# Row sums of two tiles as small products on TensorE, ordered last column blocks, and a new list of priorities

## The chip, the cores and the metric

The kernel runs on one core of one Trainium2 chip. The metric is the device time of one execution in microseconds (us). Three runs of the kernel before took 1046.98, 1047.38 and 1047.85 us; the median is 1047.38 us.

## What is computed

Three layers follow one another. Attention: 4 sequences of 768 positions, 8 heads of 64 columns; each chunk of 32 queries sees 8 memory slots, 16 positions to the left, its own 32 and 8 to the right, 64 slots in all.

```python
scores = scale * np.matmul(q_c, k_full.transpose(0, 1, 3, 2))
scores = scores - np.max(scores, axis=-1, keepdims=True)
a = np.exp(scores)
a = a / (np.sum(a, axis=-1, keepdims=True) + 1e-09)
out[:, :, c_start:c_end] = np.matmul(a, v_full)
```

Then two dense layers over the 3072 x 512 result, each 512 -> 2048 -> 512:

```python
h = x @ w_in;  r = np.maximum(h, 0.0);  g = s * (r * r) + b;  x = g @ w_out      # first
h = x @ w_in2; g = h * (1.0 / (1.0 + np.exp(-1.702 * h)));    out = g @ w_out2   # second
```

## The kernel before, in words

**Tiles.** The 3072 rows are 24 attention tiles of 128 queries. A tile (`attend`, L509 and on) goes through these steps: its k, q and v are loaded (L521); TensorE computes 64 small score products (`scores`, L536); VectorE finds each row's maximum (`top`, L553) and subtracts it (`less`, L556); ScalarE takes the exponential (`exp`, L561); TensorE transposes the result in four 128x128 pieces (`turn`, L569); ScalarE or VectorE copies it to `px` (`turned`, a copy at L328); TensorE multiplies with the values, 64 small products (`values`, L597); VectorE divides by the row sums (`norm`, L602); TensorE transposes back (`back`, L611); a copy takes the high part of the number (`keep`, L328) and VectorE the residual (`left`, L628). The row sums are `total`: a reduction (L579), the addition of 1e-9 (L582) and a reciprocal (L583), all on VectorE, on the exponentials before they are transposed. Tiles 0 to 3 are done one by one at the start, later ones in pairs; one row of 128 queries holds eight sums, two heads for each of four pieces.

**Dense layers.** All matrices are split into a high and a low part, and each product is made of three. The first layer's first 16 tiles go through `step`: hidden products into `ph` (L726), the gate (L732 to L751), output products into `accA` and `accB` (L759). The first steps work on halves of 256 columns, the first of them on tiles 0 and 1, the next on tiles 2 and 3. The first layer's weights are loaded as pairs of words, put together by bit steps on ScalarE and VectorE (`words`, L444 to L468) and split (L328 for the high part, L428 for the residual). The rest of the first layer and the whole second one go through `wino`, which makes seven products in place of eight of 2x2 blocks; its output products are at L1242. The last of them, for the last block, is issued in two pieces, one for each column block (`only`), after which VectorE adds each block to what is there (`last`, L1283) and SyncE stores it.

**Order.** The order of all operations on all engines is made before the program is built: each `op` has a due time, durations on the engines that may run it, the operations it follows, and buffers that it takes. `Plan.order` places them one after another by due time, and `SHIFTS`, a list of (first operation, how many, by how much), moves due times. Where the plan leaves TensorE idle before the first output product, idle products of a cleared tile (`cold`) are put in (L1398), into a spare pair of banks of the accumulator memory; nine more such products (`warm`, L383) stand at the very start.

Of the kernel before, what the change touches and what calls it, by code (L numbers as in the profile page):

```python
# [8 lines left out]
F32 = mybir.dt.float32  # L9
# [6 lines left out]
P = 128  # L16
# [34 lines left out]
    (1612, 256, 5), (1631, 4, 2.35), (1699, 64, -7.76), (1949, 16, -5.07), (932, 16, -1.12), (2436, 1, 0.44),  # L51
    (2730, 64, -7.95), (494, 16, -2.28), (617, 1, -1.49), (277, 256, -1.21), (3339, 4, -5.47), (3114, 1, 0.41),
    (2366, 1, 0.18), (11, 256, 1.49), (2644, 4, 0.18), (1872, 64, -0.2), (1819, 256, 1.74), (1792, 64, 0.54),
    (1748, 4, -0.8), (811, 16, -0.39), (3178, 64, -0.19), (1893, 1, 3.68), (1836, 16, -0.51), (2342, 256, 1.22),
    (586, 4, 6.05), (718, 1, -0.28), (163, 4, -0.28), (1005, 1, 2.98), (807, 1, -3.69), (2414, 1, -0.31),
    (1125, 16, 9.26), (2154, 256, -5.84), (2762, 4, -0.29), (1303, 16, 0.6), (1999, 16, -0.13), (2173, 16, 2.02),
    (26, 1, -8.88), (2170, 256, 8.5), (661, 16, -0.26), (400, 1, 10.24), (2178, 256, -1.34), (174, 256, 0.29),
    (134, 1, 2.37), (1826, 1, -0.12), (1408, 64, -4.02), (3376, 1, -8.4), (1390, 64, 0.99), (533, 1, 11.29),
    (3346, 190, -0.03), (1751, 16, -4.82), (1002, 4, 0.43), (2961, 16, -5.97), (866, 1, 5.95), (2455, 1, 0.71),
    (2840, 16, 0.37), (2154, 1, 2.59), (1139, 64, -6.74), (2904, 4, -1.42), (3397, 1, -1.7), (2313, 1, 0.2),  # L60
    (735, 256, 2.52), (2432, 4, -0.29), (1090, 1, 4.94), (1555, 16, -17.14), (56, 4, 0.91), (2969, 16, 1.88),
    (1680, 1, -0.19), (1510, 256, 12.15), (1265, 16, -6.14), (3127, 1, 0.01), (541, 64, 1.59), (545, 64, 0.39),
    (3220, 16, -3.41), (832, 4, 1.02), (1732, 64, -0.3), (295, 16, 0.5), (3353, 1, -0.07), (169, 16, -1.93),
    (2542, 1, -7), (571, 1, -0.78), (930, 16, 1.9), (1956, 4, -0.67), (829, 4, -5.41), (3219, 1, -1.84),
    (1547, 16, -7.23), (687, 64, 6.82), (2974, 256, -0.53), (2700, 1, 0.08), (1878, 4, -1.83), (588, 4, 4.82),
    (2496, 1, -0.32), (630, 256, -0.9), (942, 1, 0.01), (1754, 16, -0.05), (1295, 1, 0.35), (488, 4, 0.68),
    (52, 16, -0.37), (3529, 7, -0.92), (2015, 4, -0.39), (1956, 1, -0.08), (2924, 1, -2.32), (1156, 16, -7.77),
    (2844, 16, 2.35), (177, 1, 3.67), (50, 1, -0.46), (591, 64, -1.01), (856, 1, -3.3), (1006, 1, 0.8),
    (2193, 1, -0.41), (1372, 64, 15.19), (485, 4, 3.62), (672, 1, 3.48), (2030, 4, 0.07), (1474, 4, 1.64),
    (2478, 16, -2.66), (3007, 256, 3.34), (272, 1, -2.45), (2452, 1, -0.46), (900, 1, -3.84), (2024, 256, -3.55),  # L70
    (3270, 256, 0.54), (91, 1, -4.78), (1423, 1, 5.39), (2014, 1, 11.48), (1053, 1, 0.14), (2198, 256, -0.21),
    (1768, 16, 3.5), (2254, 1, -1.34), (722, 1, 4.56), (895, 1, -0.86), (1290, 1, -1.23), (1546, 1, -1.37),
    (2311, 16, 11.12), (1200, 1, 15.34), (863, 1, -0.4), (291, 16, 2.64), (3258, 16, 1.92), (3273, 16, 4.73),
    (1726, 4, -0.36), (2745, 1, -2.35), (2473, 64, 0.01), (1200, 4, 2.13), (2860, 64, 1.9), (3408, 128, 0.27),
    (2952, 1, 1.67), (3033, 16, 6.88), (985, 1, -10.64), (1180, 4, -10.28), (1714, 16, 0.31), (2727, 1, -0.98),
    (1961, 64, -11.04), (1888, 64, -3.48), (2164, 1, 0.4), (933, 4, 1.23), (1005, 1, 9.03), (1568, 256, -2.38),
    (1989, 256, -1.22), (499, 4, 0.83), (2385, 1, -6.17), (610, 4, -1.31), (1250, 16, 5.62), (655, 1, 11.83),
    (3443, 93, 0.22), (1326, 256, -1.49), (498, 1, 0.41), (1667, 64, 5.33), (1797, 256, 0.03), (1155, 1, -20.91),
    (2379, 16, -1.41), (2101, 256, 11.19), (2234, 16, -0.24), (1835, 1, 1.88), (3409, 4, 0.21), (3, 4, -9.87),
    (634, 64, -1.41), (425, 1, 3.76), (899, 4, -15.64), (2121, 1, 3.25), (1645, 1, 2.15), (43, 256, -0.21),  # L80
    (3152, 64, -15.49), (2815, 64, -0.61), (2367, 16, 1.67), (63, 256, -0.26), (800, 1, 19.59), (2835, 16, 1.94),
    (426, 16, -4.3), (2965, 16, 0.96), (1667, 256, 11.64), (174, 64, 2.81), (795, 1, -1.21), (2316, 256, 9.24),
    (2389, 16, -1.62), (3184, 256, -0.7), (1421, 64, -2.34), (2254, 16, 0.37), (80, 4, 2), (2972, 256, -3.98),
    (1302, 4, 0.3), (1751, 1, 0.29), (245, 1, 0.35), (480, 4, 1.53), (3273, 1, 0.77), (3301, 64, -2.33),
    (3310, 16, -2.39), (890, 64, -10.03), (941, 4, 3.21), (3309, 227, -0.12), (3305, 1, -5.09), (2282, 16, -0.03),
    (3002, 256, 5.54), (3291, 245, -0.4), (1884, 4, -1.75), (1457, 256, -0.29), (86, 64, -1.33), (2836, 1, 0.23),
    (468, 1, -0.65), (2000, 256, -0.82), (2323, 256, 0.31), (1866, 16, 0.88), (311, 1, 0.59), (72, 16, -13.18),
    (301, 256, -1.7), (1495, 64, -15.18), (106, 16, -9.62), (2998, 256, -10.32), (1203, 4, -0.12), (711, 16, 0.51),
    (2941, 16, 7.51), (2426, 4, -4.62), (2322, 1, -0.14), (1625, 16, -1.68), (2214, 16, 10.14), (1162, 64, -0.26),
    (394, 16, -14.55), (3295, 1, 11.77), (93, 1, -0.12), (2705, 1, -6.51), (2579, 4, 9.15), (2820, 16, -8.49),  # L90
    (2855, 1, 0.62), (953, 1, 1.8), (1438, 1, -9.09), (3351, 64, -9.1), (3389, 4, 0.41), (3484, 52, 1.11),
    (159, 64, -7.43), (735, 4, -1.72), (2740, 4, 3.76), (945, 1, -0.31), (1350, 64, 0.21), (2547, 1, 0.15),
    (3506, 30, -1.86), (2385, 4, 9.5), (3455, 16, -1.31), (1034, 4, 3.08), (2651, 4, -0.12), (1099, 1, 0.12),
    (222, 16, 2.76), (876, 1, 1.39), (2089, 256, 1.17), (2940, 16, -10.33), (278, 1, 0.71), (1063, 16, 0.45),
    (1791, 1, -1.41), (2919, 16, 0.54), (2902, 4, -0.45), (851, 16, 0.78), (3343, 1, 0.62), (1308, 1, -0.35),
    (2886, 16, -0.79), (1046, 4, -8.74), (740, 1, 5.36), (80, 1, 10.95), (1607, 1, -6.38), (2004, 64, -0.09),
    (1235, 1, 0.18), (1880, 1, 3.01), (1640, 1, -5.04), (828, 64, -0.31), (1947, 16, 1.9), (2898, 1, -0.51),
    (2407, 64, 2.44), (3100, 1, 2.11), (3202, 64, -0.68), (1363, 4, 0.12), (265, 16, -0.61), (2830, 1, -0.07),
# [193 lines left out]
def attention_moe_moe(ctx: ExitStack, tc: tile.TileContext, q_t, k_w, v_w, w_in1, w_out1, s_b, w_in2, w_out2, out):  # L292
# [32 lines left out]
    T = {}  # L325
# [39 lines left out]
    def chill(e):  # L365
        T["cold"] = pp.tile([P, KT, 512], F32, tag="ys", name="cold")[:, 0].bitcast(F32R)
        fill(e, T["cold"].bitcast(F32), 0.0)
# [1089 lines left out]
```

## Time and profile before

| what | us |
|---|---|
| median of three runs | 1047.38 |
| the profiled execution, its whole time | 1048.4 |
| its span, first to last instruction | 1046.4 |
| TensorE busy with products | 1034.9 |
| VectorE busy | 756.7 |
| ScalarE busy | 603.8 |

One execution was recorded. The span leaves out 2.0 us of the execution's time around it. TensorE is PE, and PEld its weight loads; VectorE is DVE, ScalarE ACT, GpSimd POOL, SyncE SP. A line such as L597 is a line of the kernel; L328 is a helper that many copies share. An idle time in brackets stands before an instruction, with what ended it; "issue" means that nothing in the profile ended it. [...]

### The profile page before, as it was taken

What the parts mean: (1) busy time and instruction counts of PE and PEld (TensorE: products, weight loads), DVE (VectorE), ACT (ScalarE), POOL (GpSimd) and SP (SyncE); (2) the same over time, 40 slices, a digit from 0 to 9 for tenths busy, and PEclk for the clock granted to TensorE, in tenths of its full rate; (3) what the DMA queues carried; (4) which work ended last, traced back from release to release, by engine and by line L of the source; (5) the groups of instructions that cost most, each with busy time, mean ns of one, the idle gap of its engine ahead of it and who ended that gap; (6) DMA issues with size and microseconds to landing.
All of it is one profiled execution on the core that took longest, in us unless ns stands there. A gap on an engine that the chain in (4) does not pass through costs nothing.

```text
span 1046.4 us, 19645 instructions
## 1 busy us (share of the span) xinstructions
PE 1034.9 (99%) x7563; PEld 850.8 (81%) x7563; DVE 756.7 (72%) x1144; ACT 603.8 (58%) x933; POOL 0.7 (0%) x6
## 2 busy tenths in 40 slices
PE   7999999999999999999999999999999999999998
PEld 5888888888888888888888888888888888888886
DVE  7996997879898758889999365896323996222955
ACT  5766765546666657788845476553354543454432
POOL 0000000000000000000000000000000000000000
PEclk9999999999999999999999999999999999999999
DMA  9679955748899964988978998877666677566662
GB/s 351 234 262 329 296 181 184 257 178 272 294 338 360 350 209 180 324 291 284 372 221 283 346 295 293 277 243 242 211 201 196 213 254 229 175 202 217 204 214 88
DMA packets 148605, 265.55 MB, mean 254 GB/s; under 512 B 14240, under 2 KB 59552, under 8 KB 148512
## 3 DMA queue, kind: packets, MB, share of 16 engines
q1 hardware_dynamic: 148224, 263.77, 75.2%
q8 instruction: 60, 0.98, 0.4%
q10 hardware_dynamic: 288, 0.52, 0.2%
q14 instruction: 33, 0.27, 0.1%
HBM read 190.84 MB, written 73.40 MB: 253 GB/s over the span
## 4 chain that ended last, share of the span: by engine, by line
PE 80%; DVE 4%; DMA 3%; issue 0%; ACT 0%; SPq 0%; DVEq 0%
PE pc L1242 12%; PE ph L726 9%; PE pb L1242 8%; PE pd L1242 8%; PE accA L759 5%; PE accB L759 5%; PE ph L1093 3%; PE pd L1093 3%; PE ph L1095 3%; PE pd L1095 3%; PE ph L1094 3%; PE pd L1094 3%; PE pb L1094 2%; PE pb L1093 2%; PE pc L1093 2%; PE pc L1094 2%
## 5 line engine op out<-in xcount | busy, mean ns | idle before, releaser
L1215 ACT CAST oj<-G 128x1024 fp32r<-128x1024 f32 x72 | 75.6, 1054 | 75.4 <-PE pd L1242 31.1
L1218 DVE TENSOR_TENSOR oj<-G,oj 128x1024 fp32r<-128x1024 f32 x72 | 87.6, 1220 | 40.4 <-ACT oj L1215 40.4
L732 ACT ACTIVATE r<-ph 128x512 f32<-128x512 f32 (+1 forms) x66 | 38.5, 583 | 61.8 <-PE ph L726 38.1
L1218 DVE TENSOR_TENSOR oq<-G,oq 128x1024 fp32r<-128x1024 f32 x40 | 48.9, 1222 | 30.0 <-ACT oq L1215 29.8
L1215 ACT CAST oq<-G 128x1024 fp32r<-128x1024 f32 x40 | 42.1, 1053 | 47.4 <-PE pc L1242 21.9
L1242 PE MATMUL pc<-oj,wih 128*128 128x512 f32 x224 | 69.0, 389 | 0.0
L1105 ACT ACTIVATE G<-ys 128x512 f32<-128x512 f32 x64 | 40.4, 631 | 36.5 <-DVE ys L1147 35.9
L1242 PE MATMUL pd<-oj,wih 128*128 128x512 f32 x192 | 59.1, 389 | 0.0
L1227 DVE TENSOR_TENSOR G<-G 128x1024 f32<-128x1024 f32 x48 | 57.3, 1218 | 0.1
L747 ACT CAST gh<-r 128x512 fp32r<-128x512 f32 (+1 forms) x66 | 39.9, 605 | 25.2 <-PE accB L759 15.1
L751 DVE TENSOR_TENSOR gl<-r,gh 128x512 fp32r<-128x512 f32 (+1 forms) x66 | 44.2, 669 | 14.2 <-ACT gh L747 11.2
L450 ACT ACTIVATE u<-st 128x512 f32<-128x512 f32 x64 | 42.9, 670 | 17.1 <-DMA st<-w_in 9.7
L1242 PE MATMUL pb<-oj,wih 128*128 128x512 f32 x160 | 49.3, 389 | 0.0
L1242 PE MATMUL pc<-oq,wih 128*128 128x512 f32 x160 | 49.3, 389 | 0.0
L1242 PEld LDWEIGHTS pc<-oj,wih 128*128 128x128 f32 x224 | 42.1, 188 | 8.7
L462 DVE SCALAR_TENSOR_TENSOR u<-u,st 128x512 uint32<-128x512 uint32 x64 | 43.5, 687 | 2.8 <-ACT st L458 1.5
L458 ACT ACTIVATE st<-st 128x512 uint32<-128x512 uint32 x64 | 42.8, 672 | 1.8 <-DMA st<-w_out 1.0
L468 DVE SCALAR_TENSOR_TENSOR u<-st,u 128x512 uint32<-128x512 uint32 x64 | 43.4, 683 | 0.4
L1242 PE MATMUL pc<-oj,wil 128*128 128x512 f32 x112 | 43.6, 389 | 0.0
L1242 PEld LDWEIGHTS pd<-oj,wih 128*128 128x128 f32 x192 | 36.0, 188 | 7.4
L759 PE MATMUL accA<-gh,woh 128*128 128x512 f32 (+1 forms) x132 | 42.0, 393 | 0.0
L739 ACT ACTIVATE r<-r 128x512 f32<-128x512 f32 (+1 forms) x66 | 40.8, 618 | 1.6
(229 smaller groups left out, 2735.2 us busy)
## 6 DMA issues: line engine op xcount, KB each, us to landing
wih<-wodh SPq DMA_DIRECT2D x112, 256.0 KB, 3.6
wil<-wodl SPq DMA_DIRECT2D x112, 256.0 KB, 3.9
wih<-wch SPq DMA_DIRECT2D x96, 256.0 KB, 3.6
wil<-wcl SPq DMA_DIRECT2D x96, 256.0 KB, 3.9
st<-w_in SPq DMA_DIRECT2D x32, 512.0 KB, 6.2
st<-w_out SPq DMA_DIRECT2D x32, 512.0 KB, 5.8
k<-k_w SPq DMA_DIRECT2D x24, 512.0 KB, 6.1
v<-v_w SPq DMA_DIRECT2D x24, 512.0 KB, 6.5
```

Source lines behind the costliest of these rows:

```text
L462: nc.vector.scalar_tensor_tensor(out=u, in0=u, scalar=3, in1=T["st", i][:, :, 0], op0=ALU.logical_shift_left, op1=ALU.bitwise_or)
L468: nc.vector.scalar_tensor_tensor(out=u, in0=T["st", i][:, :, 1], scalar=0x80000000, in1=u, op0=ALU.bitwise_and, op1=ALU.bitwise_or)
L726: nc.tensor.matmul(T["ph", i], T[win][x][:, k * P:(k + 1) * P], T["x", m, b][y][:, k, r], start=seen_["hid"] == 1, stop=seen_["hid"] == 3 ...
L751: nc.vector.tensor_tensor(out=gl, in0=T["r", i], in1=gh.bitcast(F32), op=ALU.subtract)
L759: nc.tensor.matmul(T["acc", group, k // 2][:, k % 2][:, r], T[wout][x][:, k * P:k * P + P], T["g", i][y], start=fresh and (x, y) == (0, 0) ...
L1093: nc.tensor.matmul(ph, wh, xh, start=first and i == 0, stop=False, skip_group_check=True)
L1094: nc.tensor.matmul(ph, wh, xl, start=False, stop=False, skip_group_check=True)
L1095: nc.tensor.matmul(ph, wl, xh, start=False, stop=i == 1, skip_group_check=True)
L1215: nc.scalar.copy(out=T[kh], in_=g_of(ty, z))
L1218: nc.vector.tensor_tensor(out=T[kl], in0=g_of(ty, z), in1=T[kh].bitcast(F32), op=ALU.subtract)
L1227: o_raw[out, x] = [op(need, {"dve": 1.22}, lambda e: nc.vector.tensor_tensor(out=g_of(out, z), in0=g_of(a, z), in1=g_of(b, z), op=o), afte ...
L1242: nc.tensor.matmul(acc[:, k], lt[:, z], rh, start=first and x == 0, stop=p == HALF - 1 and x == 2, skip_group_check=True)
```

## The change

For tiles 0 and 1 the row sums are not taken by VectorE. Once `px` is there, TensorE multiplies each of its four pieces with a small matrix of two columns that holds ones for one head's 64 slots each, and one more product of the identity and a matrix of eight columns of 1e-9 adds the constant; the eight columns stand in the second bank of the spare pair, tile 0's and tile 1's side by side. VectorE then takes one reciprocal. The matrix of ones is filled on GpSimd at the start, in a part of the cleared tile. The code also has a form in which the sums share the values' bank (`apart` false); with `SUMMED` as it stands it is not used. The two pieces of the last product now follow one another by a dependency. The list of priorities is the old one with its numbers moved by the three added operations, and 171 more entries. The spare pair is made at the start and not at the first idle product.

```diff
 SHIFTS = (
-    (1612, 256, 5), (1631, 4, 2.35), (1699, 64, -7.76), (1949, 16, -5.07), (932, 16, -1.12), (2436, 1, 0.44),
+    (1615, 256, 5), (1634, 4, 2.35), (1702, 64, -7.76), (1952, 16, -5.07), (935, 16, -1.12), (2439, 1, 0.44),
...
+    (2675, 256, 2.82), (2178, 16, -8.46),
 )
...
 
     parts = [(0,), (1,), (2,), (3,)] + [(t, t + 1) for t in range(4, TILES, 2)]
     SIDE = ((1,), (3,))
+    SUMMED = ((0,), (1,))
     at_a = {}
     for u in parts:
         for k, f in enumerate("STVX"):
...
     def fill(e, x, v):
         ENG[e].memset(x, v)
 
+    def pair(tag, name):
+        pool = {"accB": ps_acc, "accA": pools.get("ps_y"), "a": pools.get("ps_b")}[tag]
+        return Banks([pool.tile([P, 512], F32, tag=f"{tag}{n}", name=name) for n in range(2)])
+
     def chill(e):
-        T["cold"] = pp.tile([P, KT, 512], F32, tag="ys", name="cold")[:, 0].bitcast(F32R)
+        cold = pp.tile([P, KT, 512], F32, tag="ys", name="cold")
+        T["cold"], T["ones"] = cold[:, 0].bitcast(F32R), cold[:, 1, :10]
+        T["spare"] = pair("accB", "spare")
         fill(e, T["cold"].bitcast(F32), 0.0)
 
     def table(e):
...
         nc.scalar.activation(out=x, in_=T["cold"].bitcast(F32)[:, :1], func=AF.Exp)
 
     plan.tag("r", 1)
-    o_cold = op(-999, {"dve": 0.6}, chill, alloc=[("ys", "cold")])
+    o_cold = op(-999, {"dve": 0.6}, chill, alloc=[("ys", "cold"), ("accB", "spare")])
     plan.due[o_cold] = -1000.0
     plan.due[op(-999, {"act": 1.5}, table, after=[o_cold], uses=["cold"])] = -1000.0
+    def halves_(e):
+        nc.gpsimd.memset(T["ones"][:, :2], 0.0)
+        nc.gpsimd.memset(T["ones"][:, 2:], 1e-9)
+        for h in range(2):
+            nc.gpsimd.memset(T["ones"][64 * h:64 * h + 64, h:h + 1], 1.0)
+
+    o_ones = op(-140, {"pool": 0.9}, halves_, after=[o_cold], uses=["cold"])
     o_ident = op(-135, {"pool": 0.5}, lambda e: make_identity(nc, ident))
     o_sb = op(-60, {"sp": 0.06}, lambda e: nc.sync.dma_start(out=sb, in_=s_b))
 
...
             nc.vector.tensor_scalar_add(out=den, in0=den, scalar1=1e-9)
             nc.vector.reciprocal(out=den, in_=den)
 
+        summed = u in SUMMED
+        apart = summed and u[0] < 2
+
+        def region():
+            return T["spare"][:, 1][:, 8 * u[0]:8 * u[0] + 8] if apart else T["o", u][:, 0, 256:264]
+
+        def sums(e):
+            if not apart:
+                bank("o", u)
+            for a in range(HP):
+                nc.tensor.matmul(region()[:, 2 * a:2 * a + 2], T["px", g][:, u[0] % 2, a], T["ones"][:, :2], start=a == 0, stop=False, skip_group_check=True)
+            nc.tensor.matmul(region(), ident, T["ones"][:, 2:], start=False, stop=True, skip_group_check=True)
+
+        def inverse(e):
+            den = T["den", u] = att.tile([P, n * HP, 2], F32, tag="den", name="den", bufs=2)
+            nc.vector.reciprocal(out=den.rearrange("p x h -> p (x h)"), in_=region())
+
         def values(i):
             def fn(e):
-                if i == 0:
+                if i == 0 and (apart or not summed):
                     bank("o", u)
                 t = u[i] % 2
                 o = two("o")
...
             tt.append(op(pt, {"pe": 0.44}, turn(i), kind=2, after=[ex, o_ident] + tt, alloc=[] if i else [(tag, ("pp", u))], uses=[("qe", g)]))
         for i in ids:
             tc_.append(op(pv, {"act": 0.59, "dve": 0.69}, turned(i), after=list(tt), uses=[("pp", u)], **fresh("px")))
-        dn = op(px, {"dve": 0.5 + 0.6 * n}, total, after=[ex], alloc=[("den", ("den", u))], uses=[("qe", g)])
+        if not summed:
+            dn = op(px, {"dve": 0.5 + 0.6 * n}, total, after=[ex], alloc=[("den", ("den", u))], uses=[("qe", g)])
         lv = [op(pv, {"sp": 1.3}, load("v", v_w, t, "p a c s -> p (a c s)"), **fresh("v")) for t in u]
         o = []
+        if summed:
+            sm = op(pv, {"pe": 0.5}, sums, kind=2, after=tc_ + [o_ones, o_ident], alloc=[] if apart else [(tag, ("o", u))], uses=["spare", "cold"] if apart else ["cold"])
+            if apart:
+                dn = op(px, {"dve": 0.2}, inverse, after=[sm], alloc=[("den", ("den", u))], uses=["spare"])
         for i in ids:
-            o.append(op(pv, {"pe": V_PE}, values(i), kind=1, after=tc_ + [lv[i]] + o, alloc=[] if i else [(tag, ("o", u))], uses=[("v", g)]))
+            o.append(op(pv, {"pe": V_PE}, values(i), kind=1, after=tc_ + [lv[i]] + o + ([sm] if summed and not apart else []),
+                        alloc=[] if i or summed and not apart else [(tag, ("o", u))], uses=[("v", g)]))
+        if summed and not apart:
+            dn = op(px, {"dve": 0.2}, inverse, after=[sm] + o, alloc=[("den", ("den", u))], uses=[("o", u)])
         z = op(px, {"dve": 0.1 + 0.57 * n}, norm, after=o + [dn], uses=[("o", u), ("den", u), ("px", g)])
         bk = []
         for i in ids:
...
     o_split, o_y, o_part = {}, {}, {}
     halves = ("accA", "accB")
 
-    def pair(tag, name):
-        pool = {"accB": ps_acc, "accA": pools.get("ps_y"), "a": pools.get("ps_b")}[tag]
-        return Banks([pool.tile([P, 512], F32, tag=f"{tag}{n}", name=name) for n in range(2)])
 
 
 
...
                 d = weights_of(n, x, here + 16 * x - 0.5)
                 for p in (2 * x, 2 * x + 1):
                     if s == len(SEVEN) - 1 and n == 2 and p == HALF - 1:
-                        prev = [outer_product(n, p, here + 8 * p + only[0], key, d, prev + wait, only) for only in ((0,), (1,))]
+                        one_ = outer_product(n, p, here + 8 * p, key, d, prev + wait, (0,))
+                        prev = [one_, outer_product(n, p, here + 8 * p + 1, key, d, prev + wait + [one_], (1,))]
                     else:
                         prev = [outer_product(n, p, here + 8 * p, key, d, prev + wait)]
             o_end[n] = prev
...
         wino(s)
 
     with tc.manual_schedule():
-        idle = None
         for i, e in plan.order():
             if i is not None:
                 plan.ops[i][2](e)
                 continue
-            if idle is None:
-                idle = pair("accB", "idle")
             for _ in range(e):
-                nc.tensor.matmul(idle[:, 0], T["cold"][:, :P], T["cold"], start=True, stop=True)
+                nc.tensor.matmul(T["spare"][:, 0], T["cold"][:, :P], T["cold"], start=True, stop=True)
         for x in list(managers)[::-1]:
             managers[x].__exit__(None, None, None)
 
```

## Rows read from the trace of the kernel before

**Rows 1.** The page: busy time, TensorE in 40 slices, queue of instructions.

```profile
PE 1034.9 (99%) x7563; PEld 850.8 (81%) x7563; DVE 756.7 (72%) x1144; ACT 603.8 (58%) x933; POOL 0.7 (0%) x6
...
PE   7999999999999999999999999999999999999998
...
q8 instruction: 60, 0.98, 0.4%
```

**Rows 2.** Busy time by stretch: us, each engine, granted clock, DMA share, GB/s.

```profile
0.00:15.30 15.30, 10.56 (x221) 7.55 (x221) 8.60 (x19) 6.83 (x12) 0.70 (x6) 1.00 0.91 334
16.40:30.30 13.90, 11.75 (x310) 8.97 (x310) 13.71 (x28) 11.19 (x22) 0.00 (x0) 1.00 0.92 336
60.00:1042.60 982.60, 982.05 (x6558) 807.80 (x6556) 704.56 (x1044) 562.04 (x858) 0.00 (x0) 1.00 0.76 252
```

**Rows 3.** The idle products to 12.8 us: ns min/median/max, first and last start.

```profile
L1398 PE MATMUL idle<-cold x9: 387/397/500, 6.7 to 11.4; 128*128 128x512 f32 x9
```

**Rows 4.** Timeline 9 to 31 us: start, us, engine, line, out<-in, count, [idle before].

```profile
9.54 0.68 DVE L579 TENSOR_REDUCE den<-qe 128x8 f32<-128x512 f32 x1
...
10.25 0.17 DVE L582 TENSOR_SCALAR den<-den 128x8 f32<-128x8 f32 x1
...
10.46 0.20 DVE L583 RECIPROCAL den<-den 128x8 f32<-128x8 f32 x1
10.58 0.64 DVE L553 TENSOR_REDUCE top<-sc 128x8 f32<-128x512 f32 x1
...
12.88 0.42 PEld L569 LDWEIGHTS pp<-ident,qe 128*128 128x128 f32 x4
12.88 0.66 PE L569 MATMUL pp<-ident,qe 128*128 128x128 f32 x4
13.27 0.30 PEld L1398 LDWEIGHTS idle<-cold 128*128 128x128 f32 x2
...
13.38 0.62 ACT L328 CAST wih<-u 128x512 fp32r<-128x512 f32 x1 [0.57 <-DVE u L468]
...
13.91 0.58 ACT L328 COPY px<-pp 128x512 f32<-128x512 f32 x1
...
14.31 0.64 DVE L602 TENSOR_TENSOR px<-o,den 128x512 f32<-128x512 f32 x1
...
14.54 0.24 PE L597 MATMUL o<-v,px 64*32 64x64 f32 x1 [0.54 <-ACT px L328]
...
15.43 0.84 PE L597 MATMUL o<-v,px 64*32 64x64 f32 x63 [0.65 <-issue]
...
16.37 0.69 DVE L602 TENSOR_TENSOR px<-o,den 128x512 f32<-128x512 f32 x1 [0.83 <-ACT u L450]
...
16.98 0.68 DVE L428 TENSOR_TENSOR wil<-u,wih 128x512 fp32r<-128x512 f32 x1
...
20.07 1.60 PE L536 MATMUL sc<-k,qe 64*32 64x64 f32 x128
...
23.65 0.74 PE L726 MATMUL ph<-xh,wil 128*128 128x256 f32 x4 [0.50 <-DVE wil L428]
...
30.32 0.71 PE L726 MATMUL ph<-xh,wih 128*128 128x256 f32 x4 [0.49 <-DVE xh L328]
```

**Rows 5.** DMA traffic from 9.28 to 12.88 us.

```profile
DMA packets 431, 1.46 MB, mean 406 GB/s; under 512 B 74, under 2 KB 74, under 8 KB 431
```

**Rows 6.** DMA queues from 12.88 to 15.43 us: packets, MB, share.

```profile
q8 instruction: 1, 0.02, 2.5%
```

**Rows 7.** Loads issued at L521, 14.0 to 14.9 us: issue ns, then landing.

```profile
L521 SPq DMA_DIRECT2D qe<-q_t x2: 328/376/423, 14.0 to 14.4; - x2
...
DMA to landing us min/median/max: 5.6/5.7/5.9
```

**Rows 8.** Timeline of the end, 1041 to 1043 us.

```profile
1041.96 1.37 DVE L1283 TENSOR_TENSOR ys<-pc,ys 128x256 f32<-128x256 f32 x3 [4.67 <-PE pc L1242]
...
1042.21 0.39 PE L1242 MATMUL pc<-oq,wil 128*128 128x512 f32 x1
```

## Prediction: what the change does to the time

> **What bounds the kernel now.** I read the page first. TensorE is busy for 99% of the span and VectorE for 72%; of TensorE's 40 slices only the first shows less than 8 tenths [rows 1]. So time can be won where TensorE does not work: at the start, and behind its last product. The table by stretches says how much is there: TensorE works 10.56 of the first 15.3 us and 11.75 of the 13.90 us from 16.4 to 30.3, and then 982.05 of the 982.60 us from 60.0 to 1042.6 [rows 2]. Part of the busy start is filler too: nine idle products of the cold tile before 12.8 us alone [rows 3].
>
> Who holds TensorE back? From 16.4 to 30.3 us VectorE is busy for 13.71 of 13.90 us, ScalarE for 11.19, and the DMA engines for a share of 0.92 [rows 2]. VectorE is the tightest, with the transfers close behind. At 30.32 us the wait for the last cast of tile 3 ends, and from there TensorE runs nearly without waits [rows 4]. The question is how much earlier that point comes.
>
> **Part 1: the sums leave VectorE.** For tiles 0 and 1 the reduction (0.68 us), the addition of the constant (0.17) and the reciprocal (0.20) give way to one reciprocal of eight columns, now read out of the accumulator memory. No row shows that form. Below stand the 0.17 us of the smallest operation there; above the 0.64 us of the maxima, which read 512 columns of that memory [rows 4]. Eight columns are nearest to the old reciprocal: 0.20. VectorE is relieved of 2 x (1.05 - 0.20) = 1.70 us between 9.5 and 14.4 us (0.82 to 1.76 with the ends).
>
> What is late next? Tile 1's maxima (10.58 us) and tile 0's normalisation (14.31 us) stand right behind a sum and could come up to 0.85 us earlier. But the hidden layer needs both tiles, and tile 1 is the later one. Of its 64 value products one ran at 14.54 us and 63 at 15.43 us, behind 0.65 us of idle time that nothing in the profile released [rows 4]. What I think this is: TensorE's instruction stream. Its queue moved 60 blocks, 0.98 MB, for 15,126 loads and products, 252 a block [rows 1]. From 9.28 to 12.88 us the data queue alone moved 406 GB/s [rows 5]; one block came in 12.88 to 15.43 us [rows 6]; and the wait fell behind 221 products and 221 loads [rows 2], near the end of a second block. If so, tile 1's values cannot pass 15.4 us whatever VectorE does, and what was won before is swallowed.
>
> [...]
>
> What is left of the 1.70 us is work that was ready early and ran later. VectorE stood idle for 0.83 us before 16.37 us, so its backlog was empty then, and relief before that counts only through what it can pull ahead. Surely ready was the residual of the first input weights (16.98 us, 0.68; its high part was cast at 13.38 us) [rows 4]. The other 1.02 us depend on ScalarE handing over the next cast in time, and on the order. So between 0.68 and 1.70 us leave the stretch in which VectorE is full (0 if the transfers hold it); I take 1.0, the sure part and a third of the rest.
>
> **Part 2: what TensorE gets.** Ten small products. Each has a 128x128 load of the kind that the transposes show: four in 0.42 us, 0.105 each, and four products end 0.66 us after their start [rows 4]. Five are 0.53 us of loads and 0.77 us to the last result. Tile 0's lie around its values, where TensorE runs filler [rows 3]: nothing, 0.53 without that cover. Tile 1's come behind its copy (13.91 + 0.58 = 14.49 us) and ahead of its values: nothing if they are through before the wait of 15.43 us, 0.53 on tile 1's chain if they stand behind it. TensorE waited 0.50 us for a weights' residual at 23.65 us in any case [rows 4], which swallows that: I take 0 of 0 to 0.53. Were they put behind the values, the normalisation would wait 0.77 + 0.20 us more.
>
> The added wait is VectorE's reciprocal on these products. Queued behind it on VectorE are the normalisation and the weights' bit steps, and TensorE waits for both. At that place VectorE had 0.83 us of idle time [rows 4], so an instruction held there displaces nothing: 0, up to 0.97 if it is issued ahead of ready work. The ones are GpSimd fills at the very start; all six of its operations took 0.7 us [rows 1], and they are due at 11 us: hidden. The spare bank is the one the idle products used before.
>
> The scores' buffer is free for the next q loads when tile 1's transposes end (12.88 + 0.66 = 13.54 us), not its sum. The loads were issued from 14.0 us, so 0.46 us are the most that this gives, and they landed 5.6 to 5.9 us later in a full queue [rows 7]: nothing.
>
> **Part 3: the last blocks and the order.** Chaining the two column blocks of the last product fixes an order that the trace already has: block 0's addition starts at 1041.96, before block 1's last product at 1042.21 us [rows 8]. Zero. The priorities are the old list moved by the three new operations, and 171 more entries. No row prices an order. At best it removes TensorE's 13.90 - 11.75 = 2.15 us of idle time between 16.4 and 30.3 us [rows 2]; at worst it lands a load of the start one place later, 512 KB at 406 GB/s [rows 5], 1.29 us. With both signs in reach I take 0.
>
> **Sum.** -1.0 + 0 + 0. The profiled execution took 1048.4 us, its span of 1046.4 and 2.0 around it; the change would make it 1047.4. That execution stands 1.0 us above the median of 1047.38, from which the same microsecond comes off: **1046.4 us**.
>
> **Rivals.**
> *Hidden anyway (1047.3).* The scores of tiles 2 and 3 ran at 20.07 us, and their q loads landed at 14.0 + 5.6 = 19.6 and 14.4 + 5.9 = 20.3 us [rows 4, 7]. If tile 3's chain starts where it did, VectorE's relief is lost; 0.1 us may stay. For it: the DMA share of 0.92. Against it: VectorE's 13.71 of 13.90 us behind it [rows 2].
>
> *All of it comes through (1045.0).* If the wait at 15.43 us goes, or the new order moves it off tile 1's values, 1.70 + 0.65 = 2.35 us go. With q one load earlier in the queue another 1.29 us: 1043.7. Against it: the empty backlog before 16.37 us. [...]
>
> *Slower (1049.9).* The block boundary. In order of issue, tile 1's transposes end six instructions short of the wait (two idle products and one value product, each with its load), and tile 0's sums put ten ahead of them. With all nine earlier idle products kept, the boundary falls inside these transposes, which run at 15.43 and not at 12.88 us: 2.55 us on tile 1's copy, values and all behind. It decides from fewer than two idle products dropped; two less take four instructions off, and the transposes are through. For it: the count is tight. Against it: the products take the place of idle time, so that fillers should go.
>
> *It does not do what it says:* the sums hold up the same instructions, or the order before 30 us stays. That is the first rival's time, and in its chance.
>
> **Chances.** Forecast 0.46, with an own range of 1045.3 to 1047.0; hidden 0.23; all through 0.22; slower 0.09. A measurement of this kernel can tell about 0.2%, 2.1 us, from no change: below 1045.3 or above 1049.5. Faster takes the third case and a little of the forecast's lower end, 0.25; slower the last case and an unlucky order, 0.10; within, 0.65. The range of 1044.0 to 1049.1 leaves out the lower end of all-through (about 0.08) and most of the slow case (0.08).
>
> **What would show it.** Right: no reduction on VectorE for the first two tiles; the first input weights' residual before 16 us; the run without waits from about 29.3 in place of 30.3 us; nothing changed behind 60 us. Of the wait: idle time without a releaser again behind some 442 instructions, at about 15.4 us, whatever stands there. Wrong: the run starts at 30.3 us or later, TensorE is idle for more than 1 us behind 60 us, or tile 1's transposes come behind 15 us.

## The result: slower by 0.5%, and the profile after

The changed kernel took 1053.27 us (median of 6 runs), the kernel before 1048.26 beside it: a ratio of 1.0051, 95% interval 1.0040 to 1.0061. That is 5.0 us between the medians, and 5.3 us by the ratio and between the two profiled spans; 5.3 is used below. The forecast was 1046.4 with a range to 1049.1. It was wrong in sign.

The page of the changed kernel: TensorE's busy time, its 40 slices, the granted clock in tenths, and the queue of instructions, to be laid beside [rows 1].

```profile
PE 1040.0 (99%) x7581; PEld 856.7 (81%) x7581; DVE 753.2 (72%) x1134; ACT 606.2 (58%) x939; POOL 1.0 (0%) x10
...
PE   8999999999999999999999999999999999999998
...
PEclk8999999999999999999999999999999999999999
...
q8 instruction: 60, 0.98, 0.4%
```

VectorE lost 3.5 us of work (756.7 to 753.2). The sums are 1.7 us and four operations of that (in each of two tiles one reciprocal of 0.21 us stands for three operations of 1.05 us); six more operations of the 1144 went to ScalarE (933 to 939) with the new order. TensorE's busy time grew by 5.1 us. At this scale the page doesn't say why. The table by stretches does (columns as in [rows 2]; the last row is a stretch of its own):

```profile
0.00:15.30 15.30, 11.15 (x223) 8.34 (x224) 6.24 (x13) 6.10 (x10) 0.98 (x10) 0.96 0.90 338
16.40:30.30 13.90, 13.61 (x303) 11.78 (x305) 11.09 (x22) 8.80 (x17) 0.00 (x0) 0.72 0.78 260
60.00:1042.60 982.60, 981.21 (x6561) 807.80 (x6560) 705.85 (x1046) 567.13 (x867) 0.00 (x0) 1.00 0.76 254
...
14.00:24.20 10.20, 9.26 (x95) 7.65 (x96) 6.39 (x12) 4.02 (x8) 0.00 (x0) 0.50 0.88 310
```

From 16.4 to 30.3 us TensorE is now busy for 13.61 of 13.90 us, and VectorE, full before (13.71), for 11.09. That isn't progress: the granted clock there is 0.72 where it was 1.00, and from 14.0 to 24.2 us it is 0.50; the clock records of the two traces hold 1.00 and 0.50 and no other value. Busy time stretched, and the engine that I had called the tightest stood waiting. The timeline of the changed kernel shows what came first (columns as in [rows 4]; L637 and L638 are the new sums, L656 the values, L611 and L670 the transposes, L790 the hidden layer):

```profile
11.56 0.68 DVE L470 TENSOR_TENSOR wil<-u,wih 128x512 fp32r<-128x512 f32 x1
...
11.60 1.02 PE L637 MATMUL spare<-cold,px 128*128 128x2 f32 x8 [0.72 <-ACT px L356]
...
12.49 0.37 PE L638 MATMUL spare<-cold,ident 128*128 128x8 f32 x2
...
12.79 0.84 PE L656 MATMUL o<-v,px 64*32 64x64 f32 x63
12.89 0.21 DVE L642 RECIPROCAL den<-spare 128x8 f32<-128x8 f32 x1 [0.31 <-PE spare L638]
...
14.94 0.31 PE L656 MATMUL o<-v,px 64*32 64x64 f32 x1 [1.31 <-issue]
...
15.18 1.11 PE L611 MATMUL pp<-ident,qe 128*128 128x128 f32 x4
15.29 0.69 DVE L661 TENSOR_TENSOR px<-o,den 128x512 f32<-128x512 f32 x1 [2.19 <-PE o L656]
...
16.36 1.39 SPq L563 DMA_DIRECT2D qe<-q_t  x2
...
16.97 1.87 PE L637 MATMUL spare<-cold,px 128*128 128x2 f32 x8
...
19.21 1.19 PE L656 MATMUL o<-v,px 64*32 64x64 f32 x64
...
24.49 1.51 PE L578 MATMUL sc<-k,qe 64*32 64x64 f32 x128
...
33.22 1.03 PE L670 MATMUL xx<-ident,px 128*128 128x128 f32 x8 [1.50 <-DVE gl L815]
33.22 0.80 PEld L670 LDWEIGHTS xx<-ident,px 128*128 128x128 f32 x7 [1.31 <-issue]
...
34.92 1.22 PE L790 MATMUL ph<-xh,wih 128*128 128x256 f32 x8 [0.21 <-DVE u L496]
...
296.31 0.39 PE L823 MATMUL accB<-gh,wol 128*128 128x512 f32 x1 [0.81 <-issue]
```

Read it downward. The five products of a tile's sums stand as ten: x8 and x2, so ten loads and ten products for a tile, 1.26 us to the last result (11.60 to 12.49 + 0.37). The one wait of before, 0.65 us at 15.43 [rows 4], is now 1.31 us and has moved ahead of the last of tile 0's values; behind it stand tile 1's transposes, 15.18 and not 12.88 us. Two waits are new: 1.50 us that end at 33.22 (the VectorE instruction named as releaser, started at 32.23, writes nothing that these transposes read; the row of the loads, PEld, says "issue" for the same gap), and 0.81 us at 296.31. TensorE runs through from 34.92 in place of 30.32 us: 4.6 us, and 0.81 more at 296, which makes 5.4 of the span's 5.3 (1051.7 against 1046.4). Where do these waits lie in TensorE's stream? The same table from the span's start to just before each of them:

```profile
0.00:14.93 14.93, 10.79 (x221) 8.09 (x221) 6.22 (x12) 6.10 (x10) 0.98 (x10) 0.97 0.90 337
0.00:33.21 33.21, 27.27 (x602) 22.22 (x603) 20.73 (x40) 17.71 (x32) 0.98 (x10) 0.85 0.85 300
0.00:296.30 296.30, 288.63 (x3403) 237.98 (x3404) 242.00 (x425) 188.90 (x310) 0.98 (x10) 0.98 0.76 255
```

221 products ran ahead of the first wait, exactly as before [rows 2]; then 221 + 3 x 127 = 602, and 602 + 22 x 127.3 = 3403. 127 products with their loads are some 254 instructions, and the 60 packets of the queue of instructions make 253 each for 7581 products and as many loads. So I take each of these waits for the end of a block of the instruction stream: the place where one block's last instruction has run and the next block's first one must come. The loads and products that the change put in moved these ends to other work.

The transfers say the same. Queue q8 moved 0.98 MB in 60 packets, 16 KB each; I take each for one block. Counted with the instructions of TensorE's sequencer, which the rows leave out, 450, 1217 and 6849 instructions of the trace ran ahead of the three waits: from the first on, 3 and 25 times 256, less one. The DMA queues of the changed kernel from 12.46 to 13.48 us, and from 30.95 to 31.91:

```profile
q8 instruction: 1, 0.02, 6.3%
```

```profile
q8 instruction: 1, 0.02, 6.2%
```

From 13.49 to 14.93 us, and from 31.92 to 33.21, q8 moves nothing. So the first block of the trace had landed at 13.48 us, and the wait at the first end was over at 14.94; the fourth had landed at 31.91, and the wait at the fourth end was over at 33.22; the 26th at 294.90, and the wait at the 26th end at 296.31. In the kernel before, the first landed at 13.92 us, and its wait was over at 15.43. In the 15 kernels of this document 33 waits of over 0.5 us stand at such an end, each within one instruction of a multiple of 256 from the first; every one of them ended 1.2 to 1.6 us after the block of the same number had landed (1.51 us in the kernel before; 1.46, 1.31 and 1.41 in the changed one). After 12 us TensorE has no wait of over 0.5 us marked "issue" anywhere else.

### The profile page after: what moved, and what is told of

The parts are those of the page before. It is cut to its first block, busy times and chain, and to the rows that moved or that the text cites. A ratio compares the mean times of both kernels' runs of the same rounds, so it can differ in the third digit from the quotient of the medians.

```text
span 1051.7 us, 19689 instructions
## 1 busy us (share of the span) xinstructions
PE 1040.0 (99%) x7581; PEld 856.7 (81%) x7581; DVE 753.2 (72%) x1134; ACT 606.2 (58%) x939; POOL 1.0 (0%) x10
## 4 chain that ended last, share of the span: by engine, by line
PE 96%; DVE 1%; DMA 1%; ACT 1%; issue 0%; DVEq 0%; ACTq 0%
PE ph L790 16%; PE pc L1306 12%; PE pb L1306 8%; PE pd L1306 8%; PE accA L823 8%; PE accB L823 8%; PE ph L1157 3%; PE pd L1157 3%; PE ph L1159 3%; PE pd L1159 3%; PE ph L1158 3%; PE pd L1158 3%; PE pb L1157 2%; PE pb L1158 2%; PE pc L1157 2%; PE pc L1158 2%
## 5 line engine op out<-in xcount | busy, mean ns | idle before, releaser
L811 ACT CAST gh<-r 128x512 fp32r<-128x512 f32 (+1 forms) x66 | 40.1, 608 | 30.3 <-PE accB L823 19.3
```

## The experiments

Two helpers. "Small products" are products of the scores' form on the cold tile ahead of the warming ones; each makes two loads and two products:

```diff
+        c0 = T["cold"].bitcast(F32)
+        for i in range(CALLS):
+            z, r = slice(0, 64), slice(CH * (i % CT), CH * (i % CT) + CH)
+            nc.tensor.matmul(w[r, :64], c0[z, :CH], c0[z, :64], start=True, stop=True)
         for _ in range(WARM):
```

CALLS is their number, and WARM the number of warming products, 9 in both kernels. They shift the stream by 4 x CALLS instructions, less 2 for each warming product dropped. "Fillers" are the kernel's own idle products (two instructions each). Runs through: where the last wait of the start ends, 30.32 in the kernel before, 34.92 in the changed one.

**The order or the structure?** The changed kernel with the priorities of before:

```diff
-        for at, n, by in SHIFTS:
+        for at, n, by in SHIFTS[:392]:
```

> The changed kernel with the first 392 entries of its priority list alone: the sums on TensorE, without the 171 new entries. Theory 'stream' (a block boundary of TensorE's instruction stream falls behind 442 loads and products, TensorE stands still there until about 15 us, and the granted clock falls): the sums add forty instructions ahead of the boundary with the old list too, so a wait without releaser of 0.6 us or more behind 442 instructions, ending near 15 us, and 1049 to 1054 us in all. Rival 'order' (the new list itself puts tile 1 late): no such wait moved ahead of tile 1's transposes, and 1047 to 1048 us.

```profile
15.16 1.11 PE L611 MATMUL pp<-ident,qe 128*128 128x128 f32 x4 [1.85 <-issue]
```

1061.78 us, 1.0133 [1.0118, 1.0149], above both forecasts. A wait of 1.85 us stood ahead of tile 1's transposes, one of 1.24 us at 34.34, and the clock was 0.50 from 15.0 to 25.2. Behind 400 us TensorE was idle for 8.4 us, against 3.4 in the kernel before; its long waits there are for ScalarE and VectorE, and none is at a block's end. The new priorities are worth 8.5 us to this structure; the new order isn't what costs 5 us.

**Where the first block ends.** The kernel before with 3 small products (12 instructions), WARM 9:

> The kernel before with three small products (twelve instructions) ahead of the warm products. Theory 'stream': the boundary behind 442 instructions now falls inside tile 1's transposes, of which the last start at about 15.4 in place of 12.9 us; 2 to 5 us slower than before, the upper end if the granted clock falls as well. Rival 'order', in which the idle time at 15.43 us is not tied to the count: within 0.5 us of before, and the wait stays in tile 1's values.

```profile
13.20 0.33 PE L573 MATMUL pp<-ident,qe 128*128 128x128 f32 x1 [0.74 <-ACT qe L565]
14.67 0.49 PE L573 MATMUL pp<-ident,qe 128*128 128x128 f32 x3 [1.14 <-issue]
```

The wait moved by 12 instructions and now cuts tile 1's transposes, where my slow rival has it. Its price is nothing that can be measured: 1048.44 us, 1.0005 [0.9995, 1.0015]. The rival's place was right here and its 2.55 us were not. Why a wait of 1.14 us costs so little here stays open.

**The first block's end taken away from the changed kernel.** 16 small products, WARM 8 (a shift of 62):

> The changed kernel with 16 small products of the scores' form (64 instructions) put ahead of the warm products, and one warm product less: 62 instructions more at the start, nothing else moved. Theory 'stream': the first boundary is now passed in tile 0's scores near 6.3 us, its block is asked for 2.5 us earlier, and there is no wait without releaser above 0.4 us before 18 us; tile 1's transposes run by 14.3 us in place of 15.2; the granted clock stays at 1.00; 1047.5 to 1049.5 us against 1053. Rival 'order': 1052 to 1054 us, with tile 1's transposes where they were.

```profile
28.43 0.26 PE L582 MATMUL sc<-k,qe 64*32 64x64 f32 x1 [3.29 <-issue]
```

1057.34 us, 1.0091 [1.0072, 1.0110]: worse. The wait of 14.94 is gone, one of 3.29 us at the end of the scores of tiles 2 and 3 (28.43 us) took its place, with 1.06 at 84 us and 0.58 at 325, and the clock fell to 0.50 all the same (13.5 to 23.7 us, again from 27.1). One end moved means all ends moved.

**The clock by itself.** The kernel before with its fillers cut to 64 columns:

```diff
-                nc.tensor.matmul(idle[:, 0], T["cold"][:, :P], T["cold"], start=True, stop=True)
+                nc.tensor.matmul(idle[:, 0, :64], T["cold"][:, :P], T["cold"][:, :64], start=True, stop=True)
```

> The kernel before with its idle products made of 64 columns and not 512: the same instructions in the same order, with less of TensorE's activity. If the filler is what holds the granted clock, it falls to 0.5 somewhere between 8 and 20 us for several us, and the time grows by 2 to 5 us. If the low clock of the changed kernel comes from its 1.3 us wait alone, the clock stays at 1.00 and the time within 0.5 us of before.

```profile
10.70:17.40 6.70, 5.31 (x142) 4.58 (x143) 6.24 (x13) 4.69 (x9) 0.00 (x0) 0.50 1.01 389
```

The clock is 0.50 for these 6.8 us where it was 1.00 with the fillers at full width: here they hold it up. The price: 1049.0 us, 1.0012 [1.0003, 1.0022], 1.3 us, less than the 2 to 5 expected. In that time TensorE also waited for 1.79 us for the next q, at 21.85 us.

**The clock held in the changed kernel.** Four fillers ahead of tile 0's sums, four behind its values:

> The changed kernel with four more idle products of 512 columns ahead of tile 0's sums and four more behind tile 0's values, its order otherwise the same. Theory 'clock' (the low granted clock from 14 to 24 us is the larger part of the 5 us): the clock stays at 1.00, the stand-still at the block boundary stays, and the time is 1048.5 to 1050.5 us. Rival 'path' (the ten sums' products themselves, issued as twenty because each runs in two passes, stand on tile 1's path, and the clock only follows): the clock may hold, the time is 1051.5 to 1053.5 us.

```profile
0.00:28.28 28.28, 22.76 (x475) 18.10 (x476) 18.18 (x36) 13.73 (x24) 0.98 (x10) 1.00 0.90 327
0.00:31.93 31.93, 25.02 (x602) 19.97 (x603) 19.53 (x38) 16.87 (x31) 0.98 (x10) 1.00 0.86 308
```

```profile
28.29 0.81 PE L611 MATMUL pp<-ident,qe 128*128 128x128 f32 x6 [1.89 <-issue]
29.39 1.44 PE L656 MATMUL o<-v,px 64*32 64x64 f32 x121 [0.29 <-ACT px L356]
31.94 0.31 PE L656 MATMUL o<-v,px 64*32 64x64 f32 x7 [1.11 <-issue]
```

The clock stayed at 1.00 and the time did not come back: 1054.41 us, 1.0073 [1.0056, 1.0090]. The fillers' 16 instructions put other work under the ends, which stand at 475 and 602 products, with waits of 1.12, 1.89, 1.11 and (at 295 us) 2.63 us. The lines show why it matters what a block holds: the 128 value products of two tiles are 256 instructions, as many as lie from one end to the next, and 121 of them ran in 1.44 us; TensorE went on with the next block 3.65 us after the last one (28.29 to 31.94).

**Clock held and first end moved.** The same with 26 small products, WARM 7:

> The same with 26 small products (104 instructions) at the start and two warm products less, so that the first block boundary is passed in tile 0's scores and the later ones away from the scores of tiles 2 and 3. 'Clock': no wait without releaser above 0.5 us before 30 us and the clock at 1.00: 1047.0 to 1049.0 us. 'Path': the same waits gone, but 1050 to 1052 us, with the first hidden product not before 20.5 us.

1056.01 us, 1.0082 [1.0067, 1.0097]. The start was nearly free of waits (runs through from 31.84), and waits of 3.05 us at 195 us (scores) and 2.23 at 318 took the gain. The ends matter over the whole stream.

**The products alone, in the kernel before.** Its order untouched, its own sums kept, the ten products of a tile ahead of the values of tiles 0 and 1, with no reader:

```diff
+                if u in ((0,), (1,)):
+                    c0 = T["cold"].bitcast(F32)
+                    for a in range(HP):
+                        nc.tensor.matmul(T["idle"][:, 1][:, 2 * a:2 * a + 2], T["px", g][:, u[0] % 2, a], c0[:, :2], start=a == 0, stop=False, skip_group_check=True)
+                    nc.tensor.matmul(T["idle"][:, 1][:, :8], ident, c0[:, :8], start=False, stop=True, skip_group_check=True)
```

> The kernel before, which keeps its sums on VectorE, with the same ten small products per tile put ahead of the values of tiles 0 and 1, their results unused. If the products, and what they do to the clock and the block boundary, are the cause, it is slower by 2.5 to 6 us (1050 to 1053.5), with the granted clock down near 14 us. If the new order is the cause, it stays within 1 us of before.

```profile
14.63 0.42 PE L602 MATMUL o<-v,px 64*32 64x64 f32 x3 [1.43 <-issue]
...
16.77 1.87 PE L592 MATMUL idle<-cold,px 128*128 128x2 f32 x8
...
34.81 1.11 PE L616 MATMUL xx<-ident,px 128*128 128x128 f32 x4 [2.48 <-DVE r L748]
```

1055.33 us, 1.0077 [1.0062, 1.0092]. Products that nobody waits for give the whole picture: the waits at 14.6, 34.8 and 299 us (and 0.76 at 362), the clock at 0.50 from 14.0 to 24.2 (and from 34.5 to 37.9). Sums, order and reciprocal are not needed for it.

**A shift alone, without sums.** The kernel before with 26 small products, WARM 7 (a shift of 100):

> The kernel before with 26 small products at the start and two warm products less (100 instructions more). If the idle time at 15.43 us is the wait for an instruction block, it goes: tile 1's values run in one piece from about 14.6 us, and the time is 0.3 to 0.8 us below before. If the later boundaries fall badly, or the start itself is later, it is within 0.5 us of before on the other side.

```profile
15.31 0.86 PE L601 MATMUL o<-v,px 64*32 64x64 f32 x64 [0.55 <-ACT px L328]
...
24.37 0.32 PE L540 MATMUL sc<-k,qe 64*32 64x64 f32 x8 [2.97 <-issue]
```

Tile 1's values run in one piece, so the old 0.65 us can be taken away; 2.97 us at the end of the scores of tiles 2 and 3 replace it, and 0.60, 0.58 and 1.31 come at 320, 350 and 357 us. 1055.27 us, 1.0078 [1.0061, 1.0095], for instructions that run at the very start. They put tile 0's scores at 6.37 us in place of 5.94; tile 1's stayed (9.19 and 9.17). The places of before were good ones.

**Other places for the changed kernel.** 28 small products, WARM 5; and 27, WARM 4, with three fillers ahead of tile 0's sums:

> The changed kernel with 28 small products (112 instructions) at the start and four warm products less: its block boundaries lie 104 instructions earlier in the work, in the middle of the scores and values of tiles 2 and 3 and not at their ends. Theory 'blocks' (the larger part of the 5 us are waits at block boundaries): less than 1 us of waits without releaser before 40 us, every one of them 193 instructions into a block of 256; the clock still falls near 13.5 us for 10 us, since no filler is added; TensorE runs through from 32 to 33.5 us against 34.9 in the changed kernel and 30.3 before. In all 1049 to 1052 us, later boundaries included. Rival 'clock': it runs through no earlier than 34 us.

> The same phase (27 small products, five warm products less, three more idle products in the wait ahead of tile 0's sums). If these hold the clock, the difference to the run above is the clock's price at equal block boundaries: 'blocks' expects 0.5 to 1.5 us, 'clock' 2.5 us or more. What then still lies behind 30.3 us at the point from which TensorE runs through is the path: 0.3 to 1.3 us for the products of the sums.

1054.76 us, 1.0068 [1.0051, 1.0085], and 1054.41 us, 1.0063 [1.0048, 1.0078]. In the first a wait of 2.08 us fell into tile 1's values and 3.03 into scores at 195 us, with 0.71 at 322; the second held the clock at 1.00 to 194 us and still lost 1.45, 0.73, 3.03 and 0.71 us. No gain, and no price of the clock: the block ends of the two were not equal in what they cost.

Up to here no kernel's time fell into the range that its expectation gave for the theory at test; these counted one or two block ends and not all of them.

**One whole block.** If only the places count, a shift by a whole block must undo the loss, though it adds still more instructions. First the products alone (40 instructions) with 58 small products, WARM 1: 216 + 40 = 256.

> The kernel before with the unused products ahead of the values of tiles 0 and 1, as it was run above with 7.7 us lost, and now 58 small products at the start and eight warm products less: 216 instructions, which with the 40 of the sums make one whole block, so that all boundaries behind tile 1 lie where they lie in the kernel before. 'Blocks': the waits behind 30 us go, and 1048.5 to 1051 us remain for the products and the clock. If the products themselves cost it, 1053 us or more as before.

1049.6 us, 1.0018 [1.0009, 1.0027], and no wait of over 0.5 us at a block's end left: 6.2 of its 8.1 us came back, with the same sums. The clock still fell to 0.50 for 3.4 us from 18.6, and TensorE ran through from 32.89.

Then the changed kernel, 36 instructions ahead by then: 59 small products, WARM 1 (220 + 36).

> The changed kernel with 59 small products of the scores' form at the start (two loads and two products each, 236 instructions) in place of eight of the nine warming products (16). In the trace the changed kernel runs 36 instructions more than the kernel before by the scores of the tiles behind 40 us, so 220 + 36 = 256, one whole block: block ends behind tile 1 fall where they do in the kernel before (one short of tile 1's values; 98 instructions into the scores of tiles 2 and 3; 40 into their values; in the hidden layer). Theory 'blocks': idle time without a releaser sums to under 1 us (3.62 in the changed kernel), TensorE runs through by 32.5 us at the latest (34.92), and the time is 1047 to 1050 us, nearer to the kernel before than to the changed one. Rival 'clock': the granted clock falls to 0.5 as in the changed kernel and most of the loss stays, 1051 to 1053. Rival 'the products and the order themselves': wherever the blocks lie, VectorE's queue now holds the chain up, 1052 us or more.

```profile
11.80 1.02 PE L641 MATMUL spare<-cold,px 128*128 128x2 f32 x8
...
12.99 0.86 PE L660 MATMUL o<-v,px 64*32 64x64 f32 x64
13.78 0.66 PE L615 MATMUL pp<-ident,qe 128*128 128x128 f32 x4
...
15.12 1.04 PE L641 MATMUL spare<-cold,px 128*128 128x2 f32 x8
...
16.32 0.86 PE L660 MATMUL o<-v,px 64*32 64x64 f32 x64
...
29.41 1.22 PE L794 MATMUL ph<-xh,wih 128*128 128x256 f32 x8 [0.21 <-ACT xh L356]
```

```profile
0.00:29.40 29.40, 26.02 (x722) 20.88 (x722) 21.32 (x43) 18.76 (x34) 0.98 (x10) 1.00 0.94 345
```

1048.45 us, 1.0008 [0.9996, 1.0020]: the loss is gone but for what can't be told from nothing. No wait of over 0.5 us stands at a block's end, the clock is 1.00 throughout the sums without a filler more, and TensorE runs through from 29.41 us, 0.9 us sooner than in the kernel before. The profiled run, span 1044.6, is its fastest; its 12 runs spread to 1053.58 us, wider than those of before (1047.14 to 1049.89), and what makes the long ones long was not found. So the 0.9 us at the start are those of one run, and the median shows no gain from them. The kernel before with a whole block of small products and nothing else was not run: what the start alone gives or costs by having eight warming products fewer isn't known.

Last the same with four fillers ahead of tile 0's sums and two behind its values, 56 small products:

> The same whole-block shift (56 small products for eight warming ones, 208 instructions, and 12 of six idle products: four ahead of tile 0's sums, two behind tile 0's values), so blocks as in the kernel before and TensorE kept at work around the small sums. Theory 'blocks', with the clock the smaller part: the clock stays at 1.00 from 9 us, no wait without a releaser over 0.7 us, TensorE runs through between 29.3 and 31.5 us, and the time is 1045.5 to 1048.5 us: the VectorE relief of 1.7 us can come through at last. Rival 'the products themselves cost': the two tiles' twenty loads and products each stay on the chain and the time is 1048.5 to 1051 with the clock held. Rival 'other waits': 1051 or more.

1050.17 us, 1.0013 [1.0004, 1.0022]. Again no wait of over 0.5 us at a block's end. But the trace's first clock record, 1.00, begins only at 13.6 us, where it begins at 9.1 in the run above, at 7.2 in the changed kernel and at 4.7 in the kernel before (the rows count the time ahead of it, for which the trace has no record, as 1.00). Three fillers from 11.40 us took 1.63 us, where three took 0.94 in the run above; tile 0's sums came at 14.11 and not 11.80 us, and TensorE ran through from 32.16. So this run says nothing of the price of the clock in the sums; its time lies in the range of the rival "the products themselves cost", whose condition, the clock held, it doesn't meet.

The long waits and the times, side by side (us over the kernel before = ratio less 1, times 1047.5; waits and clock as read in each kernel's one trace):

| kernel | waits at block ends over 0.5 us | us of clock 0.50 from 10 to 1000 us | over before |
|---|---|---|---|
| before | 0.65 | none | 0 |
| changed | 1.31, 1.50, 0.81 | 10.2 | 5.3 |
| changed, old list | 1.85, 1.24 | 13.7 | 13.9 |
| changed, 16 small | 3.29, 1.06, 0.58 | 17.1 | 9.5 |
| before, 3 small | 1.14, 0.78 | none | 0.5 |
| before, thin fillers | none | 6.8 | 1.3 |
| changed, fillers | 1.12, 1.89, 1.11, 2.63 | none | 7.6 |
| changed, fillers, 26 small | 0.54, 3.05, 2.23 | 6.8 | 8.6 |
| before + products | 1.43, 2.48, 1.28, 0.76 | 13.7 | 8.1 |
| before, 26 small | 2.97, 0.60, 0.58, 1.31 | 3.4 | 8.2 |
| changed, 28 small | 2.08, 3.03, 0.71 | 3.4 | 7.1 |
| changed, 27 small, 3 fillers | 1.45, 0.73, 3.03, 0.71 | 3.4 | 6.6 |
| before + products, whole block | none | 3.4 | 1.9 |
| changed, whole block | none | none | 0.8 |
| changed, whole block, fillers | none | 3.6 | 1.4 |

The waits are not the whole of a loss. With the old list left aside, in the eight kernels that lost over 5 us they make up, less the 0.65 us of before, 45% to 80% of it; how the rest divides between the clock and what else is pushed back was not taken apart.

## Why the prediction was wrong

**What bounds the kernel**: right. The start sets the time; 4.6 of the 5.3 us are lost before 35 us. The sign "nothing changed behind 60 us" failed by the 0.81 us at 296, and all three signs of being wrong came: the run starts at 34.92 us, TensorE is idle for 1.39 us from 60 to 1042.6, and tile 1's transposes stand at 15.18.

**Part 1, the sums leave VectorE**: right for VectorE; that it makes the kernel faster was not seen in any run. The reduction is gone, the reciprocal took 0.21 us (0.20 said), the first input weights' residual ran at 11.56 (before 16 said). With the blocks back in place the run starts at 29.41 us in the profiled run; "about 29.3" was the forecast. But the time that should come with it, 1.0 us less, didn't: 1.0008 [0.9996, 1.0020]. In the changed kernel VectorE waited for 2.19 us at 15.29 instead.

**Part 2, what TensorE gets: "I take 0 of 0 to 0.53". This step failed**, twice over. The ten products were costed by their time alone, and their number in the stream was put at nothing in the sum. And they are twenty products with as many loads: five stand as ten, 1.26 us where I had 0.77. By their instructions the stream was 16 ahead at tile 1's transposes (20, less two dropped fillers) and some 36 ahead by the values of tiles 2 and 3, and the ends of its blocks fell where TensorE came to them 0.15 us after, 0.19 before and 0.60 after the next block had landed (0.86 after in the kernel before): it waited for 1.31, 1.50 and 0.81 us in place of 0.65. The products alone cost 8.1 us in the kernel before; with the blocks set back by a whole one they cost 1.9. For the whole change the step is from 1.0051 to 1.0008, 4.5 of 5.3 us.

How the 4.6 us to 34.92 are made up, by the trace: from 30.32 the change itself takes 0.9 (29.41 in the whole-block run), two waits add 1.31 + 1.50, and 2.7 are left, in which the clock is at 0.50 for 10.2 us. That remainder is what those two traces differ by, not a measured price of the clock; the thin fillers alone gave 1.3 us for 6.8 us of it. The clock held without the blocks in place gave nothing back (1.0073, with other waits), the blocks in place with the clock down for 3.4 us gave most (1.0018). The blocks' ends are the cause; the clock's fall comes with them here. Why it falls was not tested by itself: with the blocks set back the same sums ran at 1.00 in the changed kernel, and the unused products of the kernel before still brought 3.4 us of 0.50.

**The slow rival**: the right mechanism, at 0.09, with the wrong place and price. I had read the wait of 15.43 us as the stream's, and in the sum used it only to cap a gain. I worked out the next end and none behind it; and the end that I did price, inside tile 1's transposes, cost 0.5 us in the run that put it there (1.6 at the end of its interval), not 2.55. The bound that I gave, two fillers dropped and the transposes are through, was the error: two did go (five became three), but the sums weigh twenty and not ten, and the end fell on tile 0's last value product, ahead of the transposes all the same.

**Part 3, the order**: for this structure zero was wrong, and to the good side: 8.5 us worse with the old list. What the new list is worth apart from where it puts the block ends was not run. The last blocks: right. From the start of the last product to the end of the span it takes 4.3 us, 4.2 before [rows 8].

Most block ends show no long wait: of some 900 in the 15 kernels, 33 show one of over 0.5 us, none of them in the three whole-block runs. But these take up to 3.3 us each, and 3.1 to 6.8 us in a kernel that lost over 5 us.

## What to carry to other kernels

Price a TensorE instruction that is off the path by its place in the stream as well as by its time: count loads and products up to each idle time that nothing released, and if these lie a whole number of blocks apart, every instruction put in ahead moves all of them. Look then at what the block ahead of each end holds. Here all 27 waits behind the first end follow a block with at least 100 products of 64 columns, and no other block ended in one; but 164 blocks of that kind ended in none, one of them 128 value products that ran from 202.26 us in the changed kernel with a whole block more. So in these kernels short products say where a wait can come, and a run says whether it does: set a wait's end beside the landing of its block on the instruction queue. And count what a product is issued as, not what the source calls it.

## What was not expected

- A float32 product of two or eight columns with a 128x128 load stands as two of each: ten took 1.26 us at a clock of 1.00, and 16.97 to 19.27 us, 2.3 us, at 0.50.
- Instructions that run at the start, from 1.45 to 3.16 us, before any data have landed (the first at 4.42 us in the kernel before), cost 8.2 us in the kernel before at a shift of 100 (two warming products dropped for them); a shift of 220, on top of the 36 that the change brings, wins 4.5 us back.
- A wait at a block's end can carry the name of an innocent instruction: 1.50 us "<-DVE gl" and 2.48 us "<-DVE r" are such waits, told by their count of products (602 and 603).
- With its fillers cut to 64 columns, all else in the same order, TensorE's clock was 0.50 from 10.7 to 17.5 us, and the time grew by only 1.3 us.
